# The last third of a filter load cut in two and issued behind two squares of the first batch, with a new written-out order of that stretch

## The chip, the cores and the metric

One NeuronCore of a Trainium2 chip. The metric is the device time of one execution in microseconds, the median of several runs. Engines are named as in the profile: PE multiplies matrices (PEld loads its weights), ACT and DVE work through vectors, POOL issues the DMAs that change the type, SP issues the other DMAs and the DMA transposes.

## What is computed

For each of 8 batches (sequence 3136, width 256, z of width 64):

```
scores = z @ z.T / S                       # [3136, 3136]
x      = u * (max(scores, 0)**2 @ v)       # [3136, 256]
x1, x2, x3 = split(x @ w_proj, 3)
conv   = irfft(rfft(x2) * rfft(filter))    # circular, along the sequence
out    = (x1 * conv * x3) @ w_out
```

The filter is the same for all batches, so it is loaded and transformed once, during batch 0.

## The kernel before

**Tiles and chunks.** The sequence is cut into 25 tiles of 128 keys (the last has 64) and, for queries, into 7 chunks (`CHUNKS`, L22: five of 512, then 256 and 320). For a batch and a chunk the kernel computes blocks of scores on PE (`score_mm`, L1633), mostly two key tiles by 512 queries in one PSUM pair; a relu on ACT (L1808) or DVE (L1810) into an `R` tile; a square on ACT (L1817) or DVE (L1819) into a bf16 tile `A_t`; and the weighing with v on PE (`weigh`, L1672), which adds up in the one accumulator `ps_o` of the chunk. Here a square is called by chunk and entry: square 2.11 is entry 11 in the list of chunk 2, always of batch 0.

**Mirrored blocks.** Scores are symmetric. A square that a later chunk needs transposed goes through a DMA transpose on SP (L1757) into a tile M (`M_t`) or M2 (`M2e_t`, `M2o_t`) and is weighed there instead of being computed again. Until that transpose has landed the `A_t` tile is taken. The pool has nine of them (L418), given out in turn, so a square waits for the tile of the ninth square before it, in the order in which they were emitted. There is one tile `M_t`.

**End of a chunk.** DVE multiplies the accumulator by the transposed u (`xe`, L1853 to L1861) into `xT_t`. There is one accumulator, so PE's next chunk can weigh only after that; what PE does in between is other work that the order puts there. Then follow the projections (`add_proj`, L1145) and the first step of the transform (`dft1`, L938), whose result SP stores to DRAM (`put`, L961).

**POOL's queue.** Behind the end of each chunk POOL waits for `xT_t` with a copy of one element (`await_x`, L560; the row "tick" of the profile) and then issues the loads of later data, which change fp32 to bf16 on the way: v and z of the next batch, u of a chunk two ahead. In batch 0 the filter's parts are among them (`load_filter`, L637; asked for at L1894 to L1900). There are three parts (L653): tiles 0 to 8 behind chunk 0, 8 to 16 behind chunk 1, 16 to 25 behind chunk 2. The third also brings the last row and `w_out`:

```
filt_cuts = ((0, 8), (8, 16), (16, NT))
...
if b == 0 and c < 3:
    filt_ld[c].deps = [(tick_, None)]
```

The filter's transform (L1117 to L1124) takes four tiles a step. Its last three steps need the third part, and the results are read back before the spectrum of batch 0.

**The order of the work.** All instructions are emitted by a planner (`Plan`, L179). PE follows `ORDER` (L44), a string with one letter for each step (S scores, W and v the two halves of a weighing, A, B, Q, G and Z transforms and projections with a for their second half). `ENGINES` (L72) says whether ACT or DVE takes a job that either could do. Which job comes next on ACT, DVE, SP and POOL, and which PSUM pair a step gets, the planner finds while the kernel is built, from costs and latencies written into it; so do the fillers, matmuls without use that keep PE at work in known gaps (`filler`, L671). Each engine works through its instructions in the order of emission.

Of the kernel before, what the change touches and what calls it, by code (L numbers as in the profile page):

```python
# [16 lines left out]
ALU = mybir.AluOpType  # L17
# [5 lines left out]
INF = float("inf")  # L23
# [47 lines left out]

ENGINES = (  # L72
    "ddadddadddddadaddaaaaddaddaaadadaaadaddadadaaaddaaadadaadaaaddadaddaadddadaddaaaaadaaddaaaaaddaaaaadaadddaaa"
    "adadadaddaadaaaaddaddaaaaaddaaadaddaaadadaaadaadaddadadadaaaddadaaaaaaaaaaaddaddaadaaadaadadaadaaddaaadaadda"
    "addaaaddaaaddaadaaadadaaddadadadaadadaaaddaaaddaaadadadaaaaadaaaaaaaaadaaaaaaaaaaddadadaaaadddadadaaaaaddaaa"
    "aaaadaaadaaaaaaaaaddaddddadaadaaaaaadaaaaadadadddaadaaaaaddadadadaaddaaaaaaadadaadadadadadadaaaadaaddadadaad"
    "aaaaaddaddaadaadaaaaaaaaadaddaaaaaaaadaddaaaaddaadaadadaaaaaaadaadaddddddadadaadaaaddaadaaaaaaaadadaaaaadadd"
    "aaaaaddaaddaaadaaddadaaaddaaaddadddaaaddddaadaadaaddaadaaaaaaaaadddadaaadaaaaaaaddaaaddadadaaddaadaadaaaaada"
    "daaadadaadaddaaaaadaadddaadaaadaaaadaaadaaaaadaaadaaadaaaaaaaaaaaaadaadaadaadaaaddaaaaaddadadaadaddaadaaadda"
    "daadaaaaadadddadaaaaddaadaaadaadaaaaaaadaaadadaaadaaadaadadaaaadaaaddaaaaaadaaaaaadaaadaaadaaadddadaadaaaaad"  # L80
    "aaaadaaaddaaaaaadaadaaddaaaddaaaaddaaddddaaddadaadadaaadadadadadaadaaddaaaaaaadaaaaadddaaaaaaaadaadadaaaaadd"
    "adaaaaaddadaaadaaaaadddaaaaadaaadadaaadaaadaddaaddaaaaaaaddddddadaaaadaadaaaaadaaaaadaaadadaaaadadaddadaadda"
    "daaaaaaaaddaaaaaadadaaadaaaaadaddaaddadaadaaaddaaaaaaadadaaaaadadaadaadadaaaadaadaddaddaaaddadadaaadaaddaaad"
    "daaaaaddaaaadddadaaaaaaaaddaaddaaaadaaadaadaadadaaaaaadadaaadaaaddaaaaaaaadaaadaddaadaaaaaaadadaddaaadaaaddd"
    "adaaaaaadddadddadaaadaaaaaadaaadaaaadaaaaaaaddaddadadaaaaaaadddddaddaaddaadaaaadaddaaaadaaaaaadaaaaaaaaaadaa"
    "d"
# [25 lines left out]
DMA_GO, DMA_DONE = {"SP": 0.3, "ACT": 0.5, "POOL": 2.0}, 2.4  # L112
LAT = {"PE": 0.22, "ACT": 0.22, "DVE": 0.19, "POOL": 0.15, "SP": 0.0}


class Slots:
# [5 lines left out]
    def take(self, now=0.0):  # L122
        self.taken += 1
        self.freed.append(None)
        return self.taken - 1

    def when(self, ahead=0):
        i = self.taken + ahead - self.n
        if i < 0:
            return 0.0  # L130
        if i >= len(self.freed) or self.freed[i] is None:
            return INF
        return self.freed[i]


class Pairs:


    def __init__(self, pairs):
        self.at, self.freed = [0.0] * pairs, self  # L140

    def when(self, ahead=0):
        return sorted(self.at)[ahead]

    def take(self, now=0.0):
        k = min(range(len(self.at)), key=lambda i: self.at[i])
        self.at[k] = INF
        return k

    def __setitem__(self, k, t):  # L150
        self.at[k] = t


class Task:


    def __init__(self, emit, cost, deps=(), takes=(), prio=0, lat=None, moves=0.0, late=0.0):
        self.emit, self.cost, self.takes, self.prio = emit, cost, list(takes), prio
        self.lat, self.moves, self.late = lat, moves, late
        self.deps = [d if isinstance(d, tuple) else (d, None) for d in deps]  # L160
        self.kids, self.frees = [], []
        self.left = len(self.deps)
        self.ready = 0.0
        self.end = None
        self.holders = 1
        self.clogs = self.far = False
        self.first, self.second, self.flip = None, None, None
        for d, _ in self.deps:
            d.kids.append(self)
# [9 lines left out]
class Plan:  # L179


    def __init__(self):
        self.free = {e: 0.0 for e in ("PE", "ACT", "DVE", "SP", "POOL")}
        self.queues = {"S": [], "Q": [], "W": [], "A": [], "B": [], "Z": [], "G": []}
        self.seconds = {"v": [], "a": []}
        self.pend = {e: [] for e in ("ACT", "DVE", "SP", "POOL")}
        self.quarters = self.parts = False
        self.flip, self.turned = 0, 0.0
        self.n = self.at = 0
        self.tasks = []  # L190
# [18 lines left out]
    def ready_at(self, task):  # L209
        if task.left:  # L210
            return INF
        t = task.ready
        seen = {}
        for s in task.takes:
            k = seen.get(id(s), 0)
            t = max(t, self.choice(s).when(k))
            seen[id(s)] = k + 1
        return t

    def choice(self, s):  # L220
        if self.spare and s is self.spare[0] and not self.queues["W"] and not self.seconds["v"]:
            return min(self.spare, key=lambda x: x.when())
        return s

    def run(self, task, engine, start):
        if engine == "PE":
# [5 lines left out]
            if n > 0:  # L232
# [5 lines left out]
                elif min(pairs) <= now:  # L238
                    self.filler(pairs.index(min(pairs)), n)
# [1698 lines left out]
```

## Time and profile before

| | us |
|---|---|
| runs of the kernel | 953.29, 952.20, 948.98; median 952.20 |
| profiled execution | 947.53 |
| its span, first to last instruction | 945.8 |
| busy: PE / DVE / ACT / POOL | 920.9 / 836.6 / 825.5 / 200.8 |
| mean granted clock of PE | 0.995 |

The views used are the page; the table of windows, which gives for each stretch its length, the busy time of PE, PEld, DVE, ACT and POOL with counts, the granted clock of PE (1.00 is full), the mean share in which the 16 DMA engines were busy (over 1 where packets of several queues overlap) and GB/s; the waits; the chain of waits that ended last; the timeline of an engine (start, length, line, tiles, and in brackets the idle time before and what ended it); and the DMA queues in a window. Queue q0 is POOL's, q1 is that of SP and ACT.

### The profile page before, as it was taken

How to read it: one execution, taken by the hardware profiler on the slowest of the kernel's cores; microseconds unless marked ns; L12 is line 12 of the kernel's file. 1: busy time of each engine (PE TensorE's matmuls, PEld its weight loads, DVE VectorE, ACT ScalarE, POOL GpSimd, SP SyncE). 2: the span in 40 equal slices, each digit the busy share in tenths (PEclk: the TensorE clock that was granted, in tenths of full speed). 3: DMA queues.
4: the chain of work that ended last, by engine and by line, in shares of the span. 5: the costliest groups of instructions: out<-in, count | busy, mean ns of one | idle time of the engine just before them, and what ended most of it. 6: DMA issues, size and time to landing. Idle time of an engine off the chain costs nothing.

```text
span 945.8 us, 29001 instructions
## 1 busy us (share of the span) xinstructions
PE 920.9 (97%) x11990; PEld 544.6 (58%) x11990; DVE 836.6 (88%) x1182; ACT 825.5 (87%) x927; POOL 200.8 (21%) x434
## 2 busy tenths in 40 slices
PE   8998999999999999999999999999999999999986
PEld 3443654557555775557655576556765566555754
DVE  8995699997999999999999779999889988799785
ACT  7785699998899898898989989999899999999672
POOL 5232303122213112212021120312212220001130
PEclk9998999999999999999999999999999999999999
DMA  9999678998999598998799998999899969798867
GB/s 152 152 176 153 146 135 161 176 191 177 181 198 173 110 209 173 207 206 165 156 208 191 204 201 175 183 178 187 173 168 187 190 124 182 172 201 143 210 204 243
DMA packets 321765, 168.40 MB, mean 178 GB/s; under 512 B 231990, under 2 KB 297334, under 8 KB 321632
## 3 DMA queue, kind: packets, MB, share of 16 engines
q1 hardware_dynamic: 290976, 128.39, 66.1%
q0 software_dynamic: 29616, 36.44, 26.1%
q8 instruction: 94, 1.54, 0.7%
q10 hardware_dynamic: 1040, 1.70, 0.6%
q14 instruction: 39, 0.32, 0.1%
HBM read 90.26 MB, written 53.35 MB: 152 GB/s over the span
## 4 chain that ended last, share of the span: by engine, by line
PE 81%; DMA 6%; DVE 6%; ACT 3%; issue 2%; SPq 2%; ACTq 0%; DVEq 0%
PE ps_o_t L472 48%; PE ps_s L472 20%; PE ps_s L1650 10%; PE ps_s L1044 3%; DMA spec<-gs_t 1%; DVE R_t L1810 1%; DMA M2e_t<-A_t 1%; DVE A_t L1819 1%; DMA spec_in_t<-spec 1%; DVE xT_t L1861 1%; ACT R_t L1808 1%; DMA specf<-s_t 1%; DMA ost_t<-in_z_dram 1%; DVE xh L1268 0%; DMA A_t<-spec 0%
## 5 line engine op out<-in xcount | busy, mean ns | idle before, releaser
L472 PE MATMUL ps_o_t<-A_t,v_t 64*128 64x512 bf16 (+4 forms) x4736 | 506.4, 354 | 0.6 <-DVE xT_t L1861 0.4
L472 PEld LDWEIGHTS <-v_t 64*128 64x128 bf16 (+1 forms) x6510 | 295.9, 98 | 209.6 <-PE ps_o_t L472 13.1
L1808 ACT ACTIVATE R_t<-ps_s 128x1024 f32<-128x1024 f32 (+4 forms) x353 | 332.1, 963 | 38.6 <-PE ps_s L1650 29.7
L1817 ACT ACTIVATE A_t<-R_t 128x1024 bf16<-128x1024 f32 (+3 forms) x283 | 276.0, 995 | 22.8 <-DVE R_t L1810 11.0
L1819 DVE TENSOR_TENSOR A_t<-R_t 128x1024 bf16<-128x1024 f32 (+4 forms) x209 | 229.7, 1116 | 15.2 <-ACT R_t L1808 12.8
L1810 DVE TENSOR_SCALAR R_t<-ps_s 128x1024 f32<-128x1024 f32 (+4 forms) x159 | 175.6, 1114 | 27.4 <-PE ps_s L1650 22.4
L1650 PE MATMUL ps_s<-zT_t 64*128 64x512 bf16 (+5 forms) x1209 | 190.9, 353 | 5.8 <-ACT R_t L1808 3.8
L561 POOL COPY tick<-xT_t 1x1 bf16<-1x1 bf16 x54 | 9.6, 178 | 636.5 <-DVE xT_t L1861 636.5
L472 PE MATMUL ps_s<-xT_t,wp 64*128 64x512 bf16 (+2 forms) x864 | 120.3, 349 | 0.5 <-ACT R_t L1808 0.4
L1650 PEld LDWEIGHTS <-zT_t 64*128 64x128 bf16 (+1 forms) x1209 | 68.0, 97 | 50.9 <-issue 6.6
L512 ACT ACTIVATE x_t<-ps_s 128x1024 bf16<-128x1024 f32 (+3 forms) x82 | 76.6, 943 | 19.8 <-PE ps_s L472 18.7
L472 PE MATMUL ps_o_t<-M_t,v_t 64*128 64x512 bf16 (+4 forms) x864 | 93.4, 352 | 0.0
L1861 DVE SCALAR_TENSOR_TENSOR xT_t<-ps_o_t,uT_t 128x256 bf16<-128x256 f32 (+2 forms) x224 | 71.3, 380 | 11.6 <-PE ps_o_t L472 5.8
L1268 DVE TENSOR_TENSOR xh<-xh,H 128x2048 bf16<-128x2048 bf16 x60 | 72.4, 1218 | 1.7 <-ACT xh L512 1.4
L1177 DVE TENSOR_TENSOR gate_t<-ps_s,x_t 128x512 bf16<-128x512 f32 (+2 forms) x106 | 60.6, 613 | 13.2 <-PE ps_s L472 9.0
L1365 DVE TENSOR_TENSOR yT_t<-ps_s,gate_t 128x1024 bf16<-128x1024 f32 (+2 forms) x52 | 56.3, 1087 | 12.7 <-PE ps_s L472 10.7
L472 PE MATMUL ps_s<-wp,xT_t 64*128 64x256 bf16 x800 | 65.3, 269 | 0.4 <-DVE s_t L516 0.2
L472 PEld LDWEIGHTS <-wp 64*128 64x128 bf16 x896 | 47.4, 94 | 30.2 <-issue 3.6
L552 POOL DMA_DIRECT2D un_t<-in_u_dram x112 | 59.7, 552 | 10.2 <-issue 6.8
L472 PE MATMUL ps_s<-wo,yT_t 64*128 64x256 bf16 x756 | 60.6, 270 | 0.9 <-DVE yT_t L1365 0.6
L571 POOL DMA_DIRECT2D v_t<-in_v_dram x112 | 58.8, 541 | 8.2 <-issue 7.0
L472 PE MATMUL ps_o_t<-M2e_t,v_t 64*128 64x512 bf16 (+2 forms) x440 | 52.0, 353 | 1.6 <-DVE xT_t L1861 1.5
(176 smaller groups left out, 881.0 us busy)
## 6 DMA issues: line engine op xcount, KB each, us to landing
out_dram<-ost_t SPq DMA_DIRECT2D x58, 256.0 KB
spec_in_t<-spec SPq DMA_DIRECT2D x56, 192.0 KB
spec<-gs_t SPq DMA_DIRECT2D x56, 192.0 KB
v_t<-in_v_dram POOLq DMA_DIRECT2D x80, 128.0 KB, 5.0
un_t<-in_u_dram POOLq DMA_DIRECT2D x80, 128.0 KB, 5.5
spec<-s_t SPq DMA_DIRECT2D x40, 256.0 KB
conv_in_t<-spec SPq DMA_DIRECT2D x34, 256.0 KB
out_dram<-ost_t POOLq DMA_DIRECT2D x10, 256.0 KB, 3.7
```

What stands on the lines that cost most here:

```text
L472: last = matmul(o[ds(i, n)], w[:, ds(i, n)], m, **kw)
L512: nc.scalar.activation(out_, in_, AF.Copy)
L552: nc.gpsimd.dma_start(out=t[ds(j * N1, N1), lo - t0 : hi - t0, :], in_=x[:, n2 : n2 + hi - lo, :])
L571: nc.gpsimd.dma_start(out=t[ds(j * N1, N1), ds(v_at(a), (b - a) * D)], in_=r[:, n2 + a - lo : n2 + b - lo, :].rearrange("p t d -> p (t d)"),)
L1177: nc.vector.tensor_tensor(g[:, :, ::-1] if h == 0 else g, p, x, ALU.mult)
L1268: nc.vector.tensor_tensor(x, x[:, 1].unsqueeze(1).to_broadcast([P, 2, 2, 2 * D]), h, ALU.mult)
L1650: matmul(o[ds(m, n)], zt[h, ds(t * P + m, n)], q, start=True, stop=True)
L1808: nc.scalar.activation(r, p, AF.Relu)
L1810: nc.vector.tensor_single_scalar(r, p, 0.0, ALU.max)
L1817: nc.scalar.activation(a, r, AF.Square)
L1819: nc.vector.tensor_tensor(a, r, r, ALU.mult)
L1861: nc.vector.scalar_tensor_tensor(x[:, ::-1] if h == 0 else x, f, inv_s2, ut, ALU.mult, ALU.mult)
```

## The change

**1. Four parts.** Tiles 16 to 25 of the filter become two parts, 16 to 20 and 20 to 25; the last still brings the last row and `w_out`. They no longer wait for the end of chunk 2. Each waits, by an empty instruction on POOL, for one square: the third part for the seventh square in the list of chunk 2 (square 2.10), the fourth for the sixth of chunk 3 (square 3.9). Chunks are counted from 0, so these are the "third" and "fourth" chunk.

```
+FILTER_AT = {2: 6, 3: 5}
...
+    def await_square(un):
+        tc.add_manual_dep(
+            nc.gpsimd.nop().ins, squares[un].ins.name, mybir.DependencyInfo(needs, reason.DATA), reason="paces the casts",
+        )
...
-        n = min(8, NT - 1 - t0)
+        n = min(t1, NT - 1) - t0
...
-    filt_cuts = ((0, 8), (8, 16), (16, NT))
+    filt_cuts = ((0, 8), (8, 16), (16, 20), (20, NT))
...
+    def ask_filter(i, tick_):
+        filt_ld[i].deps = [(tick_, None)]
+        tick_.kids.append(filt_ld[i])
+        plan.add(filt_ld[i])
...
+        if b == 0 and c in FILTER_AT and sum(x[:2] == (b, c) for x in scored[: scored.index(un)]) == FILTER_AT[c]:
+            ask_filter(c, on("POOL", lambda un=un: await_square(un), 0.1, [q_]))
...
-            if calls or b == 0 and c < 3:
+            if calls or b == 0 and c < 2:
```

**2. A script in place of the planner.** `ORDER`, `ENGINES` and the planner's clock are gone. `SCRIPT` holds every step of every engine: for PE the same letters, followed by the PSUM pair and, where there is a choice, the place in the queue; `c`, `d`, `s` and `p` with a digit for the job at that place of the list of ACT, DVE, SP and POOL; `F` with the tile and the number of fillers. At the two new loads it reads as follows (`p0` and `p1` right behind the squares are the empty instruction and the load):

```
...d0a0p0s4c1p1WS0d0...         square 2.11, ..., p0 waits for 2.10, ..., p1 third part
...d0Wp0Wc1p0d0S0d0...          p0 waits for 3.9, ..., p0 fourth part, ..., square 3.10
```

**3. The new order.** Taken apart step by step, the script has the same 2693 steps of PE as `ORDER`. They differ from step 60 to step 403, that is from chunk 1 of batch 0 to chunk 2 of batch 1; later ones are the same, in renamed PSUM pairs. 57 jobs change between ACT and DVE up to there (three more on ACT). In the stretch from chunk 2 to chunk 4 of batch 0:

| | before | after |
|---|---|---|
| POOL behind chunk 1 | second part, z, v, u | second part, v, z, u, then wait for 2.10, third part |
| POOL behind chunk 2 | third part (rest of filter), v, u, z | v, u, z, then wait for 3.9, fourth part |
| SP, by what it moves | M of 2.7, M of 2.8, M2 of 2.10, z, store, u of chunk 3, M2 of 2.11, store, M of 3.6, M of 3.8 | M of 2.7, M of 2.8, z, M2 of 2.10, store, M2 of 2.11, store, M of 3.6, store, u of chunk 3, z, M of 3.8 |
| squares from 2.11 on | 2.11, 2.12, 3.5, 3.2, 3.7, 3.6, 3.8, 3.9, 3.10, 4.1, 3.11, 4.4, 4.6, 4.7 | 2.11, 2.12, 3.2, 3.5, 3.6, 3.7, 3.8, 3.9, 3.10, 3.11, 4.1, 4.4, 4.6, 4.7 |
| PE between the last weighing of chunk 2 and the first of chunk 3 | a transpose of a table, two score steps | the same and the first half of a projection of chunk 2 |
| the same from chunk 3 to chunk 4 | second half of a filter step, one score step | both halves of that filter step, two score steps |
| fillers ahead of the first transform of the last output (batch 7) | 9 | 15 |

The other fillers are a few at the start (3, 4 and 8 before; 2, 4 and 8 after) and 5 and 3 near the end in both.

More of the change, by code (lines that the diff above doesn't have):

```diff
@@ L72 @@
[L72 to L86, printed above, removed]
@@ L120, in __init__, with take @@
         self.n, self.freed, self.taken = n, [], 0
-    def take(self, now=0.0):
+    def take(self):
         self.taken += 1
@@ L125, in take @@
         return self.taken - 1
[L127 to L151, printed above, removed]
 class Task:
@@ L162, in __init__ @@
         self.left = len(self.deps)
-        self.ready = 0.0
-        self.end = None
-        self.holders = 1
+        self.ready, self.holders = 0.0, 1
         self.clogs = self.far = False
-        self.first, self.second, self.flip = None, None, None
+        self.first, self.second, self.at, self.flip = None, None, None, 0
         for d, _ in self.deps:
@@ L207, in offer @@
             self.pend[e].append(task)
[L209 to L223, printed above, removed]
@@ L225, in run @@
-    def run(self, task, engine, start):
-        if engine == "PE":
-            gap, n, pairs = start - self.free["PE"], 0, self.spare[0].at
-            if 0 < self.free["PE"] and start < OPENING:
-                n = int(gap / FILL - 0.5)
-            elif not self.queues["S"] and not self.queues["W"] and not self.seconds["v"]:
-                n = int((gap - SPARE) / FILL) + AWAKE * task.far
-            if n > 0:
-                now, acc = self.free["PE"], self.spare[1]
-                if min(pairs) > now and acc.when() <= now:
-                    i = acc.take()
-                    self.filler(None, n)
-                    acc.freed[i] = start
-                elif min(pairs) <= now:
-                    self.filler(pairs.index(min(pairs)), n)
-        task.slots = [(s, s.take(start)) for s in map(self.choice, task.takes)]
-        cost = task.cost[engine]
-        if engine == "PE" and start < SLOW_TO:
-            cost *= 2
-        end = start + cost
-        self.free[engine] = end
-        task.end = end
-        task.emit(engine)
-        for e in task.cost:
-            if task in self.pend.get(e, ()):
-                self.pend[e].remove(task)
-        lat = LAT[engine] if task.lat is None else task.lat
-        if task.moves:
-            self.bus = max(end + DMA_GO[engine], self.bus) + task.moves
-            if task.clogs:
-                self.free[engine] = max(end, self.bus - CLOG)
-            lat = self.bus + DMA_DONE + task.late - end
-        for t, i in task.frees:
-            s, k = t.slots[i]
-            if i == 0 and getattr(t, "holders", 1) > 1:
-                t.holders -= 1
-                t.held_to = max(getattr(t, "held_to", 0.0), end + lat)
-                continue
-            s.freed[k] = max(getattr(t, "held_to", 0.0), end + lat) if i == 0 else end + lat
@@ L264, in run @@
+    def run(self, task, engine):
+        task.emit(engine)
         for kid in task.kids:
-            for d, extra in kid.deps:
-                if d is task:
-                    kid.ready = max(kid.ready, end if extra == ISSUED else end + lat + (extra or 0.0))
             kid.left -= 1
@@ L315, in go, with steps @@
[L315 to L341 removed]
+    def steps(self):
+        got, script = [], iter(SCRIPT)
+        for k in script:
+            n = {"F": 2, "S": 1, "W": 0, "v": 0, "a": 1}.get(k, 2 if k.isupper() else 1)
+            got.append((k, *(int(next(script), 36) for _ in range(n))))
+        return got
@@ new lines, in forms, with go @@
+    def forms(self, steps):
+        got, last, waiting = [False] * len(steps), "", []
+        for i, (k, *_) in enumerate(steps):
+            if k in "SWv":
+                waiting.append(i)
+            elif k not in "Fcdsp":
+                for j in waiting:
+                    got[j] = last == k == "Q"
+                got[i] = k == "Q"
+                last, waiting = k, []
+        return got
+    def go(self):
+        steps = self.steps()
+        engines = {"c": "ACT", "d": "DVE", "s": "SP", "p": "POOL"}
+        for (k, *x), self.quarters in zip(steps, self.forms(steps)):
+            if k == "F":
+                self.filler(*x)
+                continue
+            if k in engines:
+                task = self.pend[engines[k]][x[0]]
+                for e in task.cost:
+                    self.pend[e].remove(task)
+                self.run(task, engines[k])
+                continue
@@ L342, in go @@
             if k in self.seconds:
-                self.seconds[k].remove(task)
+                task = self.seconds[k].pop(x[0] if x else 0)
                 task.flip = task.first.flip ^ 1
             else:
-                self.queues[k].remove(task)
+                task = self.queues[k].pop(x[1] if x[1:] else 0)
+                task.at = x[0] if x else None
                 task.flip = self.flip if k == "W" else 0
-            self.at += 1
-            self.run(task, e, start)
+            assert not task.left, "a task comes ahead of what it needs"
@@ L350, in go @@
+            self.run(task, "PE")
             if k in "Wv":
-                self.flip, self.turned = task.flip, task.end
+                self.flip = task.flip
             if task.second is not None:
@@ L651, in load_filter @@
             nc.gpsimd.dma_start(out=wo16[:], in_=moe_w_out.rearrange("(t p) n -> p t n", p=P))
-    filt_cuts = ((0, 8), (8, 16), (16, NT))
-    filt_ld = [Task(lambda e, x=x: load_filter(*x), {"POOL": 1.6}, moves=3.3, late=4.0) for x in filt_cuts]
+    filt_cuts = ((0, 8), (8, 16), (16, 20), (20, NT))
+    filt_ld = [
+        Task(lambda e, x=x: load_filter(*x), {"POOL": 1.6}, moves=0.41 * (x[1] - x[0]), late=4.0) for x in filt_cuts
+    ]
     for x in filt_ld:
@@ L1816, in sq @@
             if e == "ACT":
-                nc.scalar.activation(a, r, AF.Square)
+                squares[un] = nc.scalar.activation(a, r, AF.Square)
             else:
-                nc.vector.tensor_tensor(a, r, r, ALU.mult)
+                squares[un] = nc.vector.tensor_tensor(a, r, r, ALU.mult)
             live[un] = A
```

224 lines of the change are left out of this document (101 added, 123 removed).

## The prediction

> **What bounds the kernel now.** First the page, then the table of windows over the whole run, then around the one hole that it shows.
>
> ```profile
> PE 920.9 (97%) x11990; PEld 544.6 (58%) x11990; DVE 836.6 (88%) x1182; ACT 825.5 (87%) x927; POOL 200.8 (21%) x434
> ```
>
> ```profile
> 72.00:74.00 2.00, 1.33 (x14) 0.49 (x9) 1.23 (x1) 0.00 (x0) 1.02 (x2) 1.00 1.59 142
> 74.00:76.00 2.00, 0.00 (x0) 0.00 (x0) 0.00 (x0) 1.31 (x2) 0.00 (x0) 0.87 1.09 212
> 76.00:78.00 2.00, 1.29 (x8) 0.54 (x9) 0.67 (x1) 2.00 (x3) 0.00 (x0) 0.50 1.61 151
> 78.00:80.00 2.00, 2.00 (x12) 0.83 (x10) 1.25 (x2) 0.52 (x1) 0.00 (x0) 0.50 1.25 184
> 80.00:82.00 2.00, 2.00 (x12) 0.89 (x10) 0.00 (x0) 0.63 (x1) 0.00 (x0) 0.50 1.65 254
> 82.00:84.00 2.00, 2.00 (x20) 0.96 (x17) 1.23 (x1) 0.67 (x1) 0.00 (x0) 0.92 0.85 183
> 86.00:88.00 2.00, 0.97 (x8) 0.32 (x10) 2.00 (x5) 2.00 (x3) 1.35 (x4) 1.00 0.00 0
> 0.00:110.00 110.00, 98.55 (x889) 46.16 (x891) 90.78 (x162) 79.62 (x90) 35.30 (x80) 0.97 0.98 159
> 200.00:900.00 700.00, 697.71 (x9376) 428.74 (x9374) 631.40 (x869) 638.20 (x720) 134.22 (x290) 1.00 0.94 181
> ```
>
> PE bounds the run: between 200 and 900 us it idles 2.3 of 700 us. Batch 0 is different: 11.5 us idle before 110, most of it at one place. At 73 us PE, DVE and ACT all stop. When PE resumes, its clock stands at 0.50 until past 82. Since all later work follows PE at 99.7%, a microsecond saved at 75 should arrive at the end nearly whole.
>
> The waits, the chain and the timelines name the cause.
>
> ```profile
> ACT A_t L1817 <- DMA M2e_t<-A_t: 4.8, 1, 4.8
> ```
>
> ```profile
> 63.93 10.68 DMA M2e_t<-A_t
> ```
>
> ```profile
> 76.71 0.58 PE L1650 MATMUL ps_s<-zT_t 64*128 64x512 bf16 x1 [3.38 <-ACT R_t L1808]
> ```
>
> The transpose of square 2.11 takes 10.68 us from issue to landing. Until then its `A_t` tile is taken. Counting back in the order of squares, the ninth before 4.1 is 2.11, so square 4.1 stands on ACT for 4.8 us, the relus behind it don't empty PSUM, and PE waits 3.38 us. Why is that transpose slow?
>
> ```profile
> 55.46 2.58 SPq L1757 DMA_TRANSPOSE M_t<-A_t  x2
> ...
> 62.58 1.30 SPq L1457 DMA_TRANSPOSE uT_t<-un_t  x1
> 63.93 1.51 SPq L1757 DMA_TRANSPOSE M2e_t<-A_t  x1
> 70.38 4.31 SPq L1757 DMA_TRANSPOSE M_t<-A_t  x1
> ```
>
> ```profile
> 63.15 1.23 POOL L645 DMA_DIRECT2D xh<-in_moe_filter_fft_dram  x2 [0.29 <-issue]
> 65.90 1.06 POOL L571 DMA_DIRECT2D v_t<-in_v_dram  x2
> 66.92 1.08 POOL L552 DMA_DIRECT2D un_t<-in_u_dram  x2
> 70.51 0.52 POOL L552 DMA_DIRECT2D zn_t<-in_z_dram  x1 [2.51 <-DMA xh<-in_moe_filter_fft_dram]
> ```
>
> ```profile
> q1 hardware_dynamic: 2445, 0.61, 95.9%
> ```
>
> ```profile
> q0 software_dynamic: 1200, 1.09, 95.1%
> q1 hardware_dynamic: 1240, 0.31, 30.9%
> ```
>
> The first queue row is of 57 to 60 us, the other two of 65 to 75. Alone, q1 moves 815 packets a microsecond; beside POOL's loads it gets 124. The transpose was issued last of its queue, behind u, just as POOL put out filter, v, u and z at once.
>
> **The change part by part.** *The stall.* In the new order the store and the M2 of 2.11 come ahead of u of chunk 3, and square 4.1 comes tenth after 2.11, so its tile is that of 2.12, which no transpose holds; it is 3.11 that needs 2.11's tile, at about 70.5. From 55 us q1 then has to move M of 2.7 and 2.8, half as much for z, M2 of 2.10, a store and M2 of 2.11: 5.5 times 256 KB. In packets of 250 bytes (0.61 MB in 2445) each is some 1024 packets, together 5632, at 815 a microsecond 6.9 us.
>
> The third part is now under way at the same time. Its square ends here (squares of the trace counted in the old order):
>
> ```profile
> 54.27 1.21 DVE L1819 TENSOR_TENSOR A_t<-R_t 128x1024 bf16<-128x1024 f32 x1
> ```
>
> So it is issued at about 56, 7 us earlier than now, with half the 2 x 256 KB of the present part's tiles (rows below). At q0's 109 KB a microsecond (1.09 MB in 10 us) 256 KB occupy 2.3 us, in which q1 loses 2.0. M2 of 2.11 is then through at 55 + 6.9 + 2.0 = 63.9, before the loads behind chunk 2 flow at about 65. I therefore let the stall go: -3.38 us. Its least is nothing (a rival below), its most all of it.
>
> *The clock.* From 76 to 82 PE was busy 5.29 us at half clock and 2.00 us at 0.92: 2.65 + 0.16 = 2.8 us that would not be lost. DVE and ACT are half idle there, so PE is what counts: -2.8 us. It hangs on the stall and comes or goes with it.
>
> *Ends of chunks.* PE waits here for the end of chunk 2 and of chunk 3:
>
> ```profile
> 63.27 0.61 PE L472 MATMUL ps_o_t<-M2o_t,v_t 64*128 64x512 bf16 x4 [0.43 <-DVE xT_t L1861]
> 86.96 1.28 PE L472 MATMUL ps_o_t<-M2e_t,v_t 64*128 64x512 bf16 x8 [1.04 <-DVE xT_t L1861]
> ```
>
> ```profile
> 82.64 0.43 PE ps_s L472 x4
> ```
>
> The order now puts half a projection (0.43, the last row) into the first wait, and half a filter step and a score step (two matmuls each, 0.21 a step by that row) into the second: -0.43 and -0.43, -0.9 together. Unless the inserted step waits itself, this is only work done earlier; at worst it is worth nothing.
>
> *The fourth part.* Square 3.9 ends at 66.8:
>
> ```profile
> 65.59 1.23 DVE L1819 TENSOR_TENSOR A_t<-R_t 128x1024 bf16<-128x1024 f32 x1
> ```
>
> so this part leaves at about 68, but behind v, u and z rather than ahead of them. What flows behind chunk 2 is, in KB for each issue:
>
> ```profile
> v_t<-in_v_dram POOLq DMA_DIRECT2D x6, 128.0 KB, 4.8
> xh<-in_moe_filter_fft_dram POOLq DMA_DIRECT2D x2, 256.0 KB, 7.5
> ...
> un_t<-in_u_dram POOLq DMA_DIRECT2D x2, 128.0 KB, 9.2
> wo<-in_moe_w_out_dram POOLq DMA_DIRECT2D x1, 128.0 KB, 9.8
> ```
>
> Two issues of v and of u, z (8 tiles, 128 KB), the filter's two, its last row (32) and `w_out` make 1312 KB, of which 1056 stay: 9.7 us at 109, until about 75 instead of 77 or later. The next transposes fall into this: M of 3.6, freed to leave when PE has used up the only `M_t`, at 70 as now. With 124 packets a microsecond until 75 and 815 after, its 1024 packets are in at about 75.5. In the new order square 4.7 is the ninth after 3.6 and comes near 74.5. The nearest row is its present wait:
>
> ```profile
> 80.45 0.63 ACT L1817 ACTIVATE A_t<-R_t 128x512 bf16<-128x512 f32 x1 [1.93 <-DMA M_t<-A_t]
> ```
>
> which cost PE nothing. Between nothing and the 3.38 of the first stall I take 1.0 us on ACT and, as 3.38 of 4.8 passed on to PE there, +0.7.
>
> *POOL's two waits.* Behind the first are queued the third part and the copy that waits for chunk 2; behind the second the fourth part and the wait for chunk 3.
>
> ```profile
> 62.69 0.18 POOL L561 COPY tick<-xT_t 1x1 bf16<-1x1 bf16 x1 [10.82 <-DVE xT_t L1861]
> ```
>
> POOL stands 10.8 us there anyway; that covers the wait and two more issues (1.23 for two). Without that cover, each microsecond of lateness would delay v and u of later chunks by as much. Nothing.
>
> *The end.* Six more fillers:
>
> ```profile
> 923.93 2.12 PE L674 MATMUL ps_o_t<-ident 128*128 128x512 bf16 x9
> 925.98 0.86 PE L472 MATMUL ps_s<-T,A_t 64*128 64x128 bf16 x16
> 928.25 0.40 PE L472 MATMUL ps_s<-T,A_t 64*128 64x128 bf16 x8 [0.50 <-DMA A_t<-spec]
> ```
>
> Nine take 925.98 - 923.93 = 2.05, so six take 1.37. The transform behind them starts at once, so its data may have been there before; the 0.50 that PE waits a little later swallows part: +0.9, between nothing (the load sets the end) and 1.4.
>
> *Rest.* The new pairs of PSUM are renamings. Three jobs more on ACT, three fewer on DVE: both have room (79.6 and 90.8 of 110 us). Nothing.
>
> Sum: -3.38 - 2.8 - 0.9 + 0.7 + 0.9 = -5.5. The profiled execution took 947.53 us and would take 942.0. It lies 0.5% below the median of the runs, 952.2, to which the sum is carried over: 946.7 us.
>
> **The rivals.** *The stall moves one transpose on.* M of 3.6 gets the service of the row of 63.93, lands at 80 and holds square 4.7. Its wait is then up to 4.8 us, PE's 1.5 to 3.3. For it: SP's issue of that transpose already took 4.31 us in the present run, and now the fourth part flows beside it. Against it: v, u and z run out earlier. The row of 86 shows that 1.04 us of idling leaves the clock at 1.00, that of 76 that 3.38 halves it; at 2.4 us I count no clock. In place of the 0.7 that gives -6.2 + 2.4 = -3.8, at the long end -2.9: 949.
>
> [...]
>
> *The third part spoils its new place.* If the store ahead of M2 of 2.11 is late, that transpose is still in the queue at 65 and then crawls at 124 packets a microsecond until 75. Square 3.11 waits from 70.5, DVE stands, and the old stall is back with its clock: only the ends of chunks are gained, less the fillers: 0, 952. For it: between 57 and 60 q1 is full (95.9%). Against it: 1.1 us of room by the sum above.
>
> [...]
>
> *u of chunk 3 comes too late: slower.* It moves behind M of 3.6 and a store, so SP issues it at about 75 instead of 62.58. The end of chunk 3 needs it; that is at
>
> ```profile
> 85.49 1.42 DVE L1861 SCALAR_TENSOR_TENSOR xT_t<-ps_o_t,uT_t 128x256 bf16<-128x256 f32 x4
> ```
>
> and would be at 85.5 - 6.2 = 79.3 without the stall. With the 10.68 of the other transpose it lands at 85.7: PE idles about 6.4 us, and the clock falls again, 2.8. -5.5 + 6.4 + 2.8 = +3.7: 956. It decides from a landing after 82 or so on. Against it: the loads should be over by 75, and 1024 packets at 815 take 1.3 us.
>
> That the change doesn't do what it says: the fourth part moves by only 5 us, so little more than a new place behind v, u and z; that is in the sum.
>
> **How the numbers follow.** A measurement of this kernel can tell about 0.5% from no change, 4.8 us. The forecast has 0.60, its own range 945 to 950 by its bounds (wait passed on 0 to 2.4, fillers 0 to 1.4, ends 0 to 0.9, which will hardly all fall to one side); about two thirds of it lies over 4.8 us of gain. The stall moved on has 0.18, the spoiled place 0.12, u too late 0.10. Faster: 0.41 of the forecast and 0.04 of the second, 0.45. Slower: 0.10 of u and 0.02 of the spoiled place, 0.12. The same: 0.43. The range leaves out the slow case and a little of the best: 943.0 to 952.5.
>
> **What would show it.** Right: filter loads at about 56 and 68; no wait of ACT on `M2e_t`; PE idle under 1 us between 70 and 80 and a clock of 1.00 from 70 to 90; the end of chunk 3 near 79; 15 fillers that end after their data have landed. Wrong: a hole of over 2 us in PE before 90, or a clock under 1.00; then the tile named by ACT's, DVE's or the `xT_t` wait says which rival it was. If the hole is gone and the time is not, something after 110 us took it back.

## The result and the profile after

The changed kernel takes 942.77 us (median of 20 runs, 938.95 to 950.51); the kernel before, measured beside it, takes 949.41 (20 runs, 942.38 to 956.57). The ratio is 0.994, with an interval of 0.9922 to 0.9959: faster by 0.6%. The forecast was 946.7 us, or 0.9942 of the median of 952.2 then known. The profiled execution of the changed kernel is one of its longer ones: 948.0 us, span 946.1. Its first batch shows the gain; two later stalls hide it.

First the windows of the changed kernel (columns as in those of before).

```profile
72.00:74.00 2.00, 2.00 (x22) 0.88 (x18) 1.22 (x1) 1.97 (x3) 0.00 (x0) 1.00 1.17 149
74.00:76.00 2.00, 2.00 (x22) 0.89 (x20) 0.00 (x0) 1.62 (x3) 0.00 (x0) 1.00 1.27 290
76.00:78.00 2.00, 2.00 (x21) 1.04 (x18) 0.88 (x2) 1.86 (x4) 0.00 (x0) 1.00 1.29 68
0.00:110.00 110.00, 102.46 (x1007) 52.95 (x1009) 90.58 (x170) 86.76 (x99) 39.37 (x89) 1.00 1.06 165
200.00:900.00 700.00, 692.30 (x9291) 422.83 (x9287) 623.84 (x861) 630.75 (x711) 134.01 (x290) 1.00 0.95 179
```

The hole at 73 is gone and the clock stays at 1.00 in this stretch: up to 110 PE idles 7.5 us instead of 11.5. But between 200 and 900 it now idles 7.7 us instead of 2.3.

A chunk's length tells more than the windows. It is the distance between the ends of two `xT_t` groups on DVE (start plus length). The first row is of before, whose next group is the row of 85.49 in the prediction; the other two are of after.

```profile
61.80 1.42 DVE L1861 SCALAR_TENSOR_TENSOR xT_t<-ps_o_t,uT_t 128x256 bf16<-128x256 f32 x4
```

```profile
61.42 1.42 DVE L1784 SCALAR_TENSOR_TENSOR xT_t<-ps_o_t,uT_t 128x256 bf16<-128x256 f32 x4 [0.21 <-PE ps_o_t L381]
...
78.35 1.42 DVE L1784 SCALAR_TENSOR_TENSOR xT_t<-ps_o_t,uT_t 128x256 bf16<-128x256 f32 x4
```

Chunk 3 of batch 0 lasted 23.7 us and lasts 16.93. By the same measure chunk 4 went from 19.98 to 18.90, chunk 6 from 11.99 to 11.58 and the next chunk from 16.34 to 16.05. With half a microsecond gained at the start, the changed kernel is 8.8 us ahead by the end of chunk 0 of batch 1.

What SP and POOL did around 60, by their timelines:

```profile
60.21 2.57 SPq L1678 DMA_TRANSPOSE M2e_t<-A_t  x1
62.87 0.53 SPq L877 DMA_DIRECT2D spec<-s_t  x1
69.97 1.23 SPq L1678 DMA_TRANSPOSE M_t<-A_t  x1
...
71.93 2.36 SPq L1373 DMA_TRANSPOSE uT_t<-un_t  x1
```

```profile
55.86 1.17 POOL L559 DMA_DIRECT2D xh<-in_moe_filter_fft_dram  x2 [4.61 <-DVE A_t L1740]
62.76 1.04 POOL L485 DMA_DIRECT2D v_t<-in_v_dram  x2 [0.27 <-issue]
67.28 1.16 POOL L559 DMA_DIRECT2D xh<-in_moe_filter_fft_dram  x2 [0.65 <-DVE A_t L1740]
79.25 0.18 POOL L470 COPY tick<-xT_t 1x1 bf16<-1x1 bf16 x1 [7.97 <-DVE xT_t L1784]
```

The M2 of 2.11 leaves at 60.21, 2.55 us ahead of the first load behind chunk 2 (62.76); before it left at 63.93, 0.78 us behind it (63.15). The filter's parts leave at 55.86 and 67.28, chunk 3 ends before 79.8. The only wait for a transposed tile left in batch 0 is one of 1.6 us, on DVE, and PE doesn't notice:

```profile
DVE A_t L1740 <- DMA M2e_t<-A_t: 1.6, 1, 1.6
```

Two rows of the chain of waits, one at 551 and one at 665, show what took the lead back in this execution:

```profile
550.75 7.04 DMA M_t<-A_t
```

```profile
664.76 7.03 DMA M_t<-A_t
```

By chunk length, chunk 6 of batch 4 took 17.35 us and chunk 6 of batch 5 took 17.23; the shortest among the profiles of this study are 12.68 and 13.02. So 8.9 us were lost in these two places, with an order of steps that both kernels share there. It is the same meeting of queues: by POOL's timeline its loads of v begin at 552.01 and 664.02. The second transpose was issued 0.74 us behind them; the first was issued 1.26 us ahead of them and was slow all the same.

### The profile page after: what moved, and what is told of

Same layout as the page of the kernel before. It is cut to its first block, busy times and chain, and to the rows that moved or that the text cites. A ratio compares the mean times of both kernels' runs of the same rounds, so it can differ in the third digit from the quotient of the medians.

```text
span 946.1 us, 29014 instructions
## 1 busy us (share of the span) xinstructions
PE 920.6 (97%) x11999; PEld 546.9 (58%) x11999; DVE 832.0 (88%) x1179; ACT 828.5 (88%) x930; POOL 201.7 (21%) x436
## 3 DMA queue, kind: packets, MB, share of 16 engines
q0 software_dynamic: 29712, 36.44, 26.4%
## 4 chain that ended last, share of the span: by engine, by line
PE 82%; DMA 7%; DVE 4%; ACT 3%; issue 1%; SPq 1%; ACTq 0%; DVEq 0%
PE ps_o_t L381 49%; PE ps_s L381 20%; PE ps_s L1571 10%; PE ps_s L960 3%; DMA M_t<-A_t 2%; ACT R_t L1729 1%; DMA uT_t<-un_t 1%; DMA M2o_t<-A_t 1%; DVE A_t L1740 1%; DVE R_t L1731 1%; DMA spec<-gs_t 1%; SPq L1678 1%; ACT x_t L421 1%; DVE xT_t L1784 1%; DMA ost_t<-in_z_dram 1%
## 5 line engine op out<-in xcount | busy, mean ns | idle before, releaser
L1729 ACT ACTIVATE R_t<-ps_s 128x1024 f32<-128x1024 f32 (+3 forms) x361 | 339.0, 964 | 32.7 <-PE ps_s L1571 24.7
L1740 DVE TENSOR_TENSOR A_t<-R_t 128x1024 bf16<-128x1024 f32 (+3 forms) x212 | 232.3, 1114 | 14.4 <-ACT R_t L1729 11.3
L1571 PE MATMUL ps_s<-zT_t 64*128 64x512 bf16 (+4 forms) x1205 | 189.8, 353 | 5.2 <-ACT x_t L421 2.4
L1731 DVE TENSOR_SCALAR R_t<-ps_s 128x1024 f32<-128x1024 f32 (+4 forms) x151 | 166.2, 1111 | 22.6 <-PE ps_s L1571 14.6
L381 PE MATMUL ps_s<-xT_t,wp 64*128 64x512 bf16 (+2 forms) x848 | 118.3, 350 | 0.5 <-ACT R_t L1729 0.2
L421 ACT ACTIVATE x_t<-ps_s 128x1024 bf16<-128x1024 f32 (+3 forms) x77 | 72.0, 944 | 20.9 <-PE ps_s L381 20.0
L381 PEld LDWEIGHTS <-wp 64*128 64x128 bf16 x896 | 47.0, 94 | 30.4 <-issue 2.6
L381 PEld LDWEIGHTS <-xT_t 64*128 64x128 bf16 x800 | 42.1, 94 | 18.8 <-issue 2.5
```

Of the source, the lines that this page charges most:

```text
L381: last = matmul(o[ds(i, n)], w[:, ds(i, n)], m, **kw)
L421: nc.scalar.activation(out_, in_, AF.Copy)
L1571: matmul(o[ds(m, n)], zt[h, ds(t * P + m, n)], q, start=True, stop=True)
L1729: nc.scalar.activation(r, p, AF.Relu)
L1731: nc.vector.tensor_single_scalar(r, p, 0.0, ALU.max)
L1740: squares[un] = nc.vector.tensor_tensor(a, r, r, ALU.mult)
```

## The experiments

The theory tested first was *order*: the sequence on SP decides, the filter's volume does not. Its rival was *volume*. What became of both is in this table. "Ahead" is the time by which the last of the early transposes (the M2 of 2.11, or u of chunk 3 where that comes after it) is issued ahead of the first load behind chunk 2; minus means behind. "Wait" is the longest single wait of a square for a transposed tile in this stretch. Each ratio is to runs of the kernel before that were measured beside that kernel, so it is not the quotient of two medians of the table.

| kernel | median us | ratio [95%] | chunk 3, chunk 4 us | ahead us | wait us |
|---|---|---|---|---|---|
| before | 949.41 | | 23.68, 19.98 | -0.8 | 4.8 |
| old order, turn first | 953.50 | 1.0043 [1.0020, 1.0066] | 24.46, 21.44 | -0.4 | 8.2 |
| old order, filter moved | 952.00 | 1.0039 [1.0011, 1.0067] | 22.88, 19.99 | -1.7 | 5.3 |
| old order, both of these | 949.23 | 1.0003 [0.9973, 1.0032] | 20.30, 22.42 | -2.5 | 4.7 |
| old order, u late | 943.85 | 0.9968 [0.9937, 0.9999] | 17.42, 19.98 | 1.5 | none |
| old order, turn first, u late | 944.46 | 0.9953 [0.9922, 0.9984] | 17.42, 19.99 | 1.2 | 0.8 |
| changed | 942.77 | 0.9940 [0.9922, 0.9959] | 16.93, 18.90 | 2.6 | 1.6 |
| changed, again | 943.44 | 0.9966 [0.9938, 0.9995] | 16.93, 20.00 | 2.6 | none |
| new order, filter back | 944.99 | 0.9958 [0.9930, 0.9987] | 16.93, 18.63 | 2.7 | 1.3 |
| new order, u first | 941.42 | 0.9939 [0.9913, 0.9964] | 16.93, 17.94 | 1.0 | none |
| new order, u first, filter back | 944.18 | 0.9963 [0.9933, 0.9993] | 16.94, 18.82 | 0.8 | 1.5 |
| new order, filter at once | 946.95 | 0.9972 [0.9949, 0.9995] | 16.95, 18.99 | 2.3 | 3.0 |
| new order, nine fillers | 943.42 | 0.9949 [0.9922, 0.9975] | 16.93, 19.23 | 2.6 | 1.9 |
| new order, u first, nine fillers | 941.52 | 0.9937 [0.9911, 0.9962] | 16.93, 18.53 | -0.6 | 1.2 |

The orders of SP below are written by what each step moves. The kernels with the old order are the code of the changed kernel with a script that holds the steps of before and, apart from the edits shown, nothing of the new order; where these edits don't reach, their chunks last as long as before (the first chunk of batch 1 takes 16.3 us in all of them, and 16.1 with the new order).

**Turn first.** The order of before, the filter in three parts.

```diff
 SP: ... M2 of 2.10, z,
+    M2 of 2.11,
     store, u of chunk 3,
-    M2 of 2.11,
     store, M of 3.6, ...
```

> The kernel before with one change: SP issues the M2 transpose of square 2.11 ahead of the store and of u of chunk 3; filter in three parts at its old place. Theory 'order' (the transpose stood behind u and so fell into POOL's loads): it starts before 63 us, is through before 66, square 4.1 doesn't wait, PE has no hole at 73, clock 1.00; 5 to 6 us less than the kernel before. Theory 'volume' (the third part's 672 KB on top of v, u and z stop the transposes): the hole of about 3 us stays at the same square or the next one; 0 to 2 us less.

The stall moved on, and grew. Square 4.1 no longer waits, but square 4.7 does, which in the old order gets the tile of 3.6. SP's timeline, the waits and the chain:

```profile
63.57 1.27 SPq L1373 DMA_TRANSPOSE uT_t<-un_t  x1
...
70.36 10.63 SPq L1678 DMA_TRANSPOSE M_t<-A_t  x2
```

```profile
ACT A_t L1738 <- DMA M_t<-A_t: 8.2, 1, 8.2
PE ps_s L381 <- ACT R_t L1729: 6.2, 1, 6.2
```

```profile
70.36 12.68 DMA M_t<-A_t
```

It is now u of chunk 3 that is issued behind the first load (63.13). The loads take longer too (v and u of the later data land 11.0 and 11.9 us after their issue, before 9.4 and 9.2), and M of 3.6 joins them at 70: in 65 to 75 SP's queue gets 101 packets a microsecond. That is the rival "the stall moves one transpose on", at 12.68 us instead of the 10.68 assumed.

**Filter moved.** The order of before, the filter in four parts as in the changed kernel.

```diff
-    filt_cuts = ((0, 8), (8, 16), (16, NT))
+    filt_cuts = ((0, 8), (8, 16), (16, 20), (20, NT))
+FILTER_AT = {2: 6, 3: 5}
```

> The kernel before with the filter's last part in two, issued behind squares 2.10 and 3.9 as in the change; every other order as before. Theory 'order': the transpose of 2.11 still starts at 65 or later beside v, u and z at 124 packets a microsecond, lands after 72 and the hole of PE stays, over 2 us; 0 to 2 us less than the kernel before. Theory 'volume': the loads behind chunk 2 are over by 71, no hole, 5 to 6 us less.

The hole stays: PE is busy 0.11 and 0.04 us in the windows from 74 and from 76, and the chain shows the old transpose at nearly its old price.

```profile
74.00:76.00 2.00, 0.11 (x2) 0.00 (x0) 0.51 (x1) 0.06 (x1) 0.00 (x0) 1.00 1.43 192
76.00:78.00 2.00, 0.04 (x2) 0.03 (x3) 0.00 (x0) 2.00 (x3) 0.00 (x0) 0.89 1.31 248
```

```profile
65.58 10.28 DMA M2e_t<-A_t
```

So neither the one swap on SP nor moving the filter is enough. The second is no clean test of the volume: the M2 of 2.11 left 1.7 us behind the first load instead of 0.8.

**The filter back, and nine fillers, in the new order.** The first takes the two edits above back (three parts, the third ahead of v, u and z) and keeps everything else of the change; the second changes one number of the script.

```diff
-    ...F3fB30...      15 fillers
+    ...F39B30...      9 fillers
```

> The changed kernel with its new order, but the filter's rest in one part behind chunk 2, ahead of v, u and z, as before. Theory 'order': no hole at square 4.1; the M transpose of 3.6 lands 1 to 3 us later and u of chunk 3 too, so the end of chunk 3 comes 1 to 3 us later than in the changed kernel; 3 to 5 us less than the kernel before. Theory 'volume': the hole of 3 us and the halved clock are back, within 1.5 us of the kernel before.

> The changed kernel with 9 fillers instead of 15 ahead of the first transform of the last output. If the fillers and not the data set the start there (forecast): 0.5 to 1.4 us less than the changed kernel, PE waiting up to 0.5 us for the next piece as in the kernel before. If the data set it: no difference, and an idle gap in place of the six fillers.

With the filter back, chunk 3 is as short as in the changed kernel, 16.93: in this order the four parts are worth nothing there. The nine fillers made no difference that the times can tell; what the six cost is worked out further down.

**A second theory.** The order theory was right, but not how it was put: one swap made it worse. In all three old-order kernels above a transpose was issued behind the first load. So the theory became *empty queue*: what counts is that no transpose is still under way when POOL's loads begin. Its rival was *squares*: the whole new order of squares and steps is needed.

**u late.** One step moved in the order of before, with the filter in three parts; then the same with the turn first as well.

```diff
 SP: ... M2 of 2.10, z, store,
-    u of chunk 3,
     M2 of 2.11, store, M of 3.6,
+    u of chunk 3,
     M of 3.8, ...
```

> The order of before, the filter in three parts, with one step of SP moved: u of chunk 3 goes behind M of 3.6, so that the M2 of 2.11 follows the store. Theory 'empty queue': the transpose of 2.11 is issued some 1.3 us earlier than before, at about 62.6, and has about 2.4 us until the loads flow at 65; alone in its queue it needs 1.3 to 2. It is in by 65 to 66, square 4.1 does not wait, the loads end by 75, and the gain is that of both moves together, 0.4 to 0.6%. If it is just too late, part of it crawls and square 4.1 waits 1 to 4 us. Rival 'squares': as before, a hole of over 2 us between 70 and 85 and a time within 0.3% of before.

> The order of before, the filter in three parts, with two steps of SP moved: the M2 of square 2.11 goes ahead of a store (as in the run with that move alone), and u of chunk 3 goes from ahead of POOL's loads to behind M of 3.6, as in the new order. Theory 'empty queue': what counts is that no transpose is under way when POOL's loads begin to flow at about 65. With 2.11 alone moved u still was, M of 3.6 came on top of it at 70, and both crawled until the loads were done at 81-82. Here the loads run alone, as in the new order with the filter moved back (last one landed at 73.7), M of 3.6 lands by 76, square 4.7 waits under 1 us, PE idles under 1 us between 70 and 85, chunk 3 ends 6 us or more ahead of before, and the time is 0.4 to 0.6% under before. Rival 'squares': the order of squares, relus and inserted steps is needed too; then square 4.7 still waits 3 us or more, the clock falls to 0.50, and the time is within 0.3% of before.

This one step takes the whole hole away. Windows of the first, the two ends from which its chunk 3 is measured, SP's timeline, then the load at which POOL stood for 4.10 us in the run with the turn first and now for 0.47:

```profile
74.00:76.00 2.00, 2.00 (x22) 0.91 (x20) 1.41 (x2) 1.26 (x2) 0.00 (x0) 1.00 1.67 191
76.00:78.00 2.00, 2.00 (x22) 0.88 (x18) 1.35 (x2) 1.17 (x2) 0.00 (x0) 1.00 0.79 205
```

```profile
61.47 1.42 DVE L1784 SCALAR_TENSOR_TENSOR xT_t<-ps_o_t,uT_t 128x256 bf16<-128x256 f32 x4
...
78.89 1.42 DVE L1784 SCALAR_TENSOR_TENSOR xT_t<-ps_o_t,uT_t 128x256 bf16<-128x256 f32 x4
```

```profile
61.32 1.30 SPq L1678 DMA_TRANSPOSE M2e_t<-A_t  x1
...
70.12 1.50 SPq L1678 DMA_TRANSPOSE M_t<-A_t  x1
71.71 1.78 SPq L1373 DMA_TRANSPOSE uT_t<-un_t  x1
```

```profile
62.82 1.23 POOL L559 DMA_DIRECT2D xh<-in_moe_filter_fft_dram  x2 [0.29 <-issue]
...
68.64 1.15 POOL L461 DMA_DIRECT2D zn_t<-in_z_dram  x2 [0.47 <-DMA xh<-in_moe_filter_fft_dram]
```

M of 3.6 leaves at 70 in both of these runs, but in the one with the turn first it met loads that took 11.0 to 11.9 us to land. Queue q0 in 65 to 75, there and with u late:

```profile
q0 software_dynamic: 1049, 0.87, 97.7%
```

```profile
q0 software_dynamic: 1470, 1.32, 82.7%
```

With u late, the loads move 1.32 MB in these 10 us, and v, u and `w_out` land 4.6 to 5.0 us after their issue; beside u they moved 0.87 MB. The times say less than the trace: 6 us would be a ratio of 0.9937, which is the end of the interval of the one run (0.9968) and well inside that of the other (0.9953).

**u first, in the new order.** The step of the last experiment taken back in the changed kernel; then also with the filter back in three parts.

```diff
 SP: ... M2 of 2.10, store,
+    u of chunk 3,
     M2 of 2.11, store, M of 3.6, store,
-    u of chunk 3,
     z, M of 3.8, ...
```

> The changed kernel with one step of SP moved back: u of chunk 3 ahead of the M2 of 2.11 and its store. Theory 'empty queue': u takes 1.3 to 2.4 us of the queue, so M2 of 2.11 is issued at 61.5 to 63 and is still under way when the loads of v, u and z begin at 64 to 65; it crawls, square 3.11, which needs its tile, waits 3 us or more on DVE, PE idles over 2 us between 68 and 80, and half of the gain or more is lost: chunk 3 ends at most 4 us ahead of before. Rival 'squares': the place of u does not matter, chunk 3 ends 7 us ahead as in the changed kernel, and the time is 0.5 to 0.7% under before.

> The new order with both of its helps taken out: u of chunk 3 ahead of the M2 of 2.11 in SP's queue, and the filter in three parts, the third ahead of v, u and z behind chunk 2, as before. Each alone cost little: with the filter back chunk 3 ended 6.4 us ahead of before, with u first 6.2. Theory 'empty queue': u first puts the M2 of 2.11 at 62.4 or later, some 1 us before POOL's loads; with the filter's part among these at once it crawls, square 3.11 (DVE) waits 3 us or more for its tile, PE idles over 2 us between 70 and 85, and chunk 3 ends at most 4 us ahead: time within 0.3% of before. Rival 'squares': the order of squares and tiles of the new script is what cures; then chunk 3 ends 6 us or more ahead, no wait of over 1.5 us, and the time is 0.4 to 0.6% under before.

Here the expectation of the empty queue failed twice, and the rival was right: nothing was lost, chunk 3 keeps 16.93 and 16.94. The profile of the second says why. SP's and POOL's rows:

```profile
60.22 1.78 SPq L1373 DMA_TRANSPOSE uT_t<-un_t  x1
62.09 1.26 SPq L1678 DMA_TRANSPOSE M2e_t<-A_t  x1
```

```profile
62.87 1.23 POOL L559 DMA_DIRECT2D xh<-in_moe_filter_fft_dram  x2 [0.29 <-issue]
```

With the same steps ahead of it in SP's queue as before, the M2 of 2.11 leaves 0.8 us ahead of the loads, not behind them as before: in the new order the squares that feed SP come sooner (M of 2.7 at 54.21 instead of 55.46, of which 0.42 us is an earlier end of chunk 1 in that execution). The two theories are one in this: the new squares gain the time that keeps the queue empty.

**Turn first and filter moved, together,** in the order of before: does the smaller volume save the swap?

> The order of before with the M2 of 2.11 ahead of a store, u of chunk 3 still ahead of POOL's loads, and the filter in four parts behind squares 2.10 and 3.9. With the turn alone moved, square 4.7 waited 8.2 us for M of 3.6; with the filter alone moved, the hole at 74 stayed. Theory 'empty queue': u of chunk 3 is still under way when the loads begin, so both crawl as without the moved filter; M of 3.6 joins them at 70 and square 4.7 waits 3 us or more; time within 0.4% of before. Rival 'volume after all': the 256 KB that are gone from the jam let u through and end the loads by 76; then square 4.7 waits under 1.5 us, chunk 3 ends 5 us or more ahead, and the time is 0.4 to 0.6% under before.

It does not. The wait is shorter than with the turn alone (4.7 us for 8.2), but u leaves 2.5 us behind the first load, and the chain and the waits show the stall:

```profile
70.92 9.15 DMA M_t<-A_t
```

```profile
ACT A_t L1738 <- DMA M_t<-A_t: 4.7, 1, 4.7
```

**The filter at once; u first with nine fillers.** The first puts all of the filter's rest behind square 2.10; the second is the fastest version so far with the smaller number of fillers.

```diff
-    filt_cuts = ((0, 8), (8, 16), (16, 20), (20, NT))
+    filt_cuts = ((0, 8), (8, 16), (16, NT))
-FILTER_AT = {2: 6, 3: 5}
+FILTER_AT = {2: 6}
```

> The changed kernel with the whole rest of the filter behind square 2.10, in three parts in all, none behind chunk 3's squares. If the early place is what is worth something, it is worth as much or more with all of it there: chunk 3 ends 7 us ahead, time 0.5 to 0.7% under before. If the early place is a burden (twice the load beside the M2 of 2.10 and 2.11 from 57 on, some 4.5 us of q0's time instead of 2.3), the M2 of 2.11 lands after 68, square 3.11 waits 3 us or more, and chunk 3 ends at most 5 us ahead.

> The fastest version so far (the changed kernel with u of chunk 3 ahead of the M2 of 2.11) with 9 instead of 15 fillers at the end. If the six fillers cost 0.7 to 0.9 as in the changed kernel's end, it is that much under the 941.4 of the version with 15, so 0.7% under before; in the profile the end goes 0.5 to 1 us faster after the last chunk than with 15, and the clock stays at 1.00 behind the fillers. If six fewer let the clock fall, a granted clock under 1.00 stands between 924 and 940, and it is slower than with 15.

With all of it there, square 3.11 waits up to 3.0 us on DVE for the M2 of 2.11, though that leaves 2.3 us ahead of v; but PE does not, and chunk 3 keeps 16.95. The time is 0.3% under before, not the 0.5 to 0.7% expected; the profile is of the fastest execution (942.69 us, median 946.95), so what the others lost is not seen. The gain of the fillers can't be seen in the last run: its end took 57.4 us from the last chunk on, against 55.8 with u first alone, because its fillers began 1.9 us later. No version with u first can be told from the changed kernel.

**The changed kernel again.**

> The changed kernel once more, to see its second half in another execution. If its stalls of about 4 us each at 551-573 and 668-681 belong to its order, they are there again and the span is about 946. If they come in some executions only, the span is 940 to 943 and at least one of them is missing; the lead at the end of batch 0 is 8 to 9 us either way.

The span is 941.3. Chunk 6 of batch 4 took 12.69 us this time, that of batch 5 took 14.80. So these stalls come in some executions. The lead at the end of batch 0 was expected at 8 to 9 us here too, and is 6.5 (8.5 in the first profile): the start took 29.48 us instead of 28.60, and chunk 4 20.00 instead of 18.90.

## Why the prediction was right, and where it was not

**The stall and its clock: right, 6.26 us for 3.38 + 2.8 = 6.18.** The kernel with u late has the order of before without the hole; its chunk 3 is 23.68 - 17.42 = 6.26 us shorter. The cause was as stated: a transpose in the queue behind POOL's loads (before, 10.68 us from issue to landing) holds the tile of a square (4.8 us of wait).

**What cures it: half right.** The prediction credited the M2 of 2.11 with leaving ahead of u. Done alone, that made the kernel slower (1.0043). u's new place behind M of 3.6 does it alone (17.42). The prediction had priced that place only as a risk, the slower rival; u left at 71.93 and no wait for it is seen. The four parts, which the sum charged with 2.0 us of q1's time, change nothing in chunk 3 with the new order (16.93 with and without).

**M of 3.6 (+0.7): wrong, it is nothing.** The failed step is "124 packets a microsecond until 75". The loads do last until 75, but they no longer fill the engines: in 71 to 73 and in 73 to 75 POOL's queue takes 31.2% and 48.5% of their time, where it took 95.1% in the row of the prediction. Queue q1 of the changed kernel in these two stretches:

```profile
q1 hardware_dynamic: 542, 0.14, 82.0%
```

```profile
q1 hardware_dynamic: 1060, 0.39, 79.4%
```

These are 271 and 530 packets a microsecond. No square waits for `M_t`. With the filter back none waits there either: the last of the loads landed at 73.7.

**Ends of chunks (-0.9): the size is right by luck, the places are partly others.** Chunk 3 is 17.42 - 16.93 = 0.49 us shorter by the new order alone, against 0.43 forecast for its end; chunk 2 lost 0.14 (18.32 to 18.46) instead of gaining 0.43. Not forecast were chunk 6 and the next chunk (0.41 and 0.29), and chunk 4, which took between 17.94 and 20.00 us in eight profiles of the new order and 19.98 or 19.99 in the old where no stall reached it. What its length hangs on stays open.

**The fillers (+0.9): right.** PE's timeline of the changed kernel:

```profile
923.43 3.41 PE L590 MATMUL ps_o_t<-ident 128*128 128x512 bf16 x15
926.89 0.86 PE L381 MATMUL ps_o_t<-T,A_t 64*128 64x128 bf16 x16
```

They start 3.46 us apart, where nine fillers took 2.05: 1.41 us for six, and the gap of 0.50 behind the first transforms is gone, so 0.9. The profiles can be compared from the end of the last chunk to the end of the span where the five fillers ahead of these begin equally late, 30.4 to 30.7 us after that chunk: five profiles with 15 fillers take 55.7 to 56.0 us, four with nine (before among them) 54.5 to 55.0.

**POOL's waits (nothing): right.** They show as 4.61 and 0.65 us in the rows above, and POOL still stands 7.97 us at the end of chunk 3.

**The total: right, but by sums that do not all show in the times.** Batch 0 gave 8.8 us in the profile, the end took 0.8, and 8.0 would be left; the medians differ by 6.6. In the second profile of the changed kernel the same sum is 6.8 less 0.7, so executions of one kernel differ by some 2 us apart from the later stalls. That forecast and result agree to 0.0002 is luck: the second set of runs gave 0.9966, the 0.7 of M of 3.6 did not come, and the gain of chunk 4 was not in the sum. The stalls in batches 4 and 5 are one place where the rest can go. In the six profiles of the old order, before included, chunks 6 of batches 4 and 5 took together 26.4 us on average, in the eight of the new order 29.1. The order of steps is the same there, stalls of up to 1.8 us are seen with the old order too, and eight and six executions are too few to say that the new order makes them longer. That stays open.

## What to carry to other kernels

Where two DMA queues share the engines, look first at the order in which things are issued at the moment when the other queue's loads begin: in this stretch, transposes issued 0.8 us or more ahead of them cost PE nothing; where one was issued 0.4 to 2.5 us behind them, it or the next took 9 to 13 us to land, in four kernels of five. A lead is no guarantee: in batch 4 one with 1.26 us took 7.04 us to land, and PE waited. If it can't leave earlier, move what is not urgent out of its queue to behind the loads, and then look at the next transpose: with the turn first the stall moved on from the M2 of 2.11 (10.68 us before) to M of 3.6 (12.68 us). Measure such a stage by a length that repeats (here a chunk, which agreed to 0.02 us between kernels), since the whole time hides it behind stalls elsewhere.

## What was not expected of the hardware

**The size of the packets.** One kernel had its M2 of 2.11 issued 0.6 us behind the first load and lost nothing (the last line of the table). The queues in 65 to 69, first of before and then of that kernel:

```profile
q0 software_dynamic: 558, 0.39, 84.0%
q1 hardware_dynamic: 534, 0.13, 26.7%
```

```profile
q1 hardware_dynamic: 1941, 0.48, 60.7%
q0 software_dynamic: 229, 0.39, 60.0%
```

POOL's loads bring the same 0.39 MB in both. Before, they begin with the filter, in packets of 0.7 KB on average; with the filter moved they begin with v, in packets of 1.7 KB, and SP's queue gets 3.6 times as many packets through. So the moved filter seems to help where the order leaves no margin; that it is the size of the packets is argued from these rows, and no run changes that alone. With the transposes later still (1.7 us and 2.5 us) it was not enough: the M2 of 2.11 took 10.28 us there all the same, and M of 3.6 took 9.15. In the kernel that lost nothing q0 also had a smaller share of the engines in 65 to 69 (60.0% for 84.0%); no row shows why.

**The clock fell at a gap of 2.35 us and not at one of 2.68.** PE's timeline of the changed kernel and the windows around it:

```profile
673.59 0.39 PE L1571 MATMUL ps_s<-zT_t 64*128 64x512 bf16 x2 [2.35 <-ACT x_t L421]
```

```profile
674.50:675.00 0.50, 0.50 (x10) 0.27 (x6) 0.50 (x1) 0.50 (x1) 0.00 (x0) 0.72 0.62 241
675.00:678.00 3.00, 3.00 (x24) 2.01 (x22) 1.85 (x2) 3.00 (x4) 0.00 (x0) 0.50 0.51 111
678.00:678.50 0.50, 0.50 (x9) 0.40 (x6) 0.00 (x0) 0.14 (x1) 0.00 (x0) 0.87 0.00 0
```

The clock halves at 674.72 (0.72 on average in a half microsecond: 0.28 us at half), when PE has been back for over a microsecond, and stays so until 678.13, for 3.41 us. A gap of 2.71 us halved it for 6.82 in the old order with turn and filter moved; one of 2.68 us left it at 1.00 in the run with nine fillers. The prediction's "at 2.4 us I count no clock" was an estimate between the 1.04 and the 3.38 of its rows, and too kind to its rival: 2.35 us did cost clock here. Worked out in the same way, the falls behind six long gaps lasted once, twice or three times 3.41 us: 3.41 behind 2.35, 3.16 and 3.85 us, 6.82 behind 2.71 and 3.38, 10.24 behind 6.22. In the 3.41 us ahead of each, PE had been idle for at least 2.1. The two falls of this execution, at 558.66 and 674.72, lie 34 times 3.41 us apart. What sets a fall off, and why the lengths come in these steps, no run shows.
